# Two chunks at a time on TensorE: order h, o, h, o, then scores of both, y of both, k times v of both, with the scores in four PSUM banks

## The chip, the cores and the metric

The kernel runs on one core of a Trainium2 chip. The metric is the device time of one execution in microseconds; the median of three runs is given. A profile of one further execution goes with it. PE is TensorE, DVE is VectorE, ACT is ScalarE, POOL is GpSimd, and SP is the engine whose queue issues nearly all DMAs here.

## The reference

A linear attention with a decaying state (RWKV-5) is followed by a feed-forward block with a SoLU and a layer norm. All is float32. Sizes: B = 4, H = 8, S = 768, D = 48; 3072 tokens of H x D = 384 features, d_ff = 1024.

```python
for t in range(S):                                   # per batch and head
    cur = einsum('bhd,bhe->bhde', u[None] * k[t], v[t])
    y[t] = einsum('bhd,bhde->bhe', r[t], state + cur)
    state = w * state + einsum('bhd,bhe->bhde', k[t], v[t])
x = y as (B * S, H * D)
h = x @ w_in                                         # 384 -> 1024
sm = exp(h - max(h)) / (sum(exp(h - max(h))) + 1e-9)
solu = h * sm
ln = (solu - mean(solu)) / sqrt(var(solu) + 1e-6) * g_ln
out = ln @ w_out                                     # 1024 -> 384
```

## The kernel before

The tokens are cut into chunks of T = 128: six per batch, four batches, so N = 24 chunks (`units`). Chunk n belongs to batch n mod 4, so two neighbouring chunks never share a state. All work is in `direct_path`; a second function, `general_path`, stands behind a flag that the checks compute and is not executed with these inputs.

The order of instructions is written out by hand (`tc.manual_schedule()`): each engine executes its own instructions in the order in which the Python code issues them. The main loop runs over i, and each iteration does steps of several chunks in a pipeline: attention of chunk i, scores of chunk i + 1, preparation of chunks i + 2 and i + 3, the first product of chunk j = i - 2 (LA = 2) and the output product of chunk l = i - 7 (LO = 5).

What one chunk needs, with the names that are used below:

- `load`: DMAs of k, r and v, on SP, with 192 KB each.
- POOL: `decay_k` makes kp (L674), `decay_r` makes rp (L681), `weigh` makes rku (L687, L688), the state's multiplication by the decay (L785), and two small steps in `deviation`.
- Turned k and r (rk): up to chunk 8 by transposes on PE (`turn_r` L710, `turn_k` L718, the copies on DVE L711 and ACT L720). From chunk 9 (FIRST = 9) as 16-bit halves: `halve_rk` splits kp on ACT (L859) and rp on DVE (L860), a transposing DMA on SP (`turn`, L834) moves them, and `join_rk` joins them on DVE (L839, rk).
- `sum_own` (DVE L692) makes own, and `diagonal` (ACT L698, eight activations) writes the diagonal of AT.
- `scores` (PE L733): 16 matmuls into the PSUM tile at (two banks), then one predicated copy into AT on DVE (L735).
- `finish`: y on PE (L760; a part from the state and rk, then a part from AT and v), the copy xT on ACT (L772), kv on PE (L778), and the state's addition on DVE (L784). The last chunk of each batch (i = 20 to 23) needs no kv.
- `ffn_in` (PE L795, 6 products with 512 columns into the two banks of h_ps, then the exponential e on ACT, L798) and `unit`: reciprocal (DVE L805), e times h (DVE L807, which reads h_ps last), two passes on ACT (L809 and the squares L810).
- `halve_ln` (ACT L845), the transposing DMA, `join_ln` (DVE L839, lnT), and `ffn_out` (PE L877, 8 products with 384 columns, copy o on ACT L879, output DMA on SP L880).

The first iterations also convert the float64 weights in 14 pieces (`load_weights` L506, `convert_a` to `convert_d`). Later, the pieces are loaded again for a check of their size: `load_weights` on SP, then `check_words` in the next iteration, an absolute value on ACT (mag, L558) and a minimum on DVE (least, L560). Before the change, one piece is handled in each iteration from i = 12 on. `check_range` reads w once and compares it on DVE (L641 to L644). `check_sums` combines all checks ahead of the last output product; its product n_ps (L658) goes to PE.

[...]Before, at has two, h_ps two, and four single-bank buffers of pool psM rotate over turned r, turned k, o_ps, y_ps and kv_ps. Halves and reloaded pieces share one SBUF pool tag with six buffers (raw).

In the main stretch (i from 8 on) the order on PE is h, o, scores, y, kv:

```python
        if not early:
            if j < N and not early_h:
                ffn_in(j)
            if i + 2 < N:
                diagonal(i + 2)
            if j < N and not early_h:
                unit(j)
            if l == N - 1:
                check_sums()
            ffn_out(l)
        if 0 <= i + 1 < N:
            scores(i + 1)
        ...
        if 0 <= i < N:
            finish(i)
```

Of the kernel before, what the change touches and what calls it, by code (L numbers as in the profile page):

```python
# [399 lines left out]
def direct_path(  # L400
# [28 lines left out]
    T = 128  # L429
# [20 lines left out]
    psH = ctx.enter_context(tc.tile_pool(name="psH", bufs=1, space=PSUM))  # L450
    psM = ctx.enter_context(tc.tile_pool(name="psM", bufs=4, space=PSUM))

# [32 lines left out]
    for i in range(NLD):  # L485
        nc.vector.memset(kpads[i][:, :, D:P], 0.0)
        nc.vector.memset(rpads[i][:, :, D:P], 0.0)
    pss = psA.tile([128, 2, HP, T], F32, name="at")
    nc.vector.memset(pss, 0.0)

# [125 lines left out]

    def turn_table(table, out):
        ps = psM.tile([128, HP, 128], F32, tag="m", name="kd_ps")
        for a in range(HP):
            nc.tensor.transpose(ps[:, a, :], table[:, a, :], ident)  # L620
        nc.scalar.copy(out=out, in_=ps)  # L621
# [49 lines left out]
    def decay_k(i):  # L671
        X = live.setdefault(i, {})
        X["kp"] = apool.tile([128, H, P], F32, name="kp", bufs=4)
        nc.gpsimd.tensor_mul(X["kp"].rearrange("p h d -> p (h d)"),  # L674
                             kpads[i % NLD].rearrange("p h d -> p (h d)"),
                             kdec.rearrange("p a d -> p (a d)"))
# [29 lines left out]
    def turn_r(i):  # L706
        rT = factors(i)["rT"]
        ps = psM.tile([128, HP, T], F32, tag="m", name="tr_ps")
        for a in range(HP):
            nc.tensor.transpose(ps[:, a, :], pair(rpads[i % NLD], a), ident)  # L710
        nc.vector.tensor_mul(rT, ps, fore)  # L711

    def turn_k(i):
        X = live[i]
        ps = psM.tile([128, HP, T], F32, tag="m", name="tk_ps")

        for a in range(HP):
            nc.tensor.transpose(ps[:, a, :], pair(X["kp"] if i > 0 else kpads[0], a), ident)  # L718
        if i > 0:
            nc.scalar.copy(out=X["kT"], in_=ps)  # L720
        else:
            nc.vector.tensor_mul(X["kT"], ps, back)
# [3 lines left out]
    def scores(i):  # L726
        X = live[i]
        A4 = X["AT"].rearrange("p (a q) t -> p q a t", q=2)
        for a in range(HP):
            for c in range(2):  # L730
                for q in range(2):
                    rows = slice(q * P, q * P + D)
                    nc.tensor.matmul(pss[ts(c, P), q, a, c * P :], X["kT"][rows, a, ts(c, P)],  # L733
                                     X["rT"][rows, a, c * P :], start=True, stop=True)
        nc.vector.copy_predicated(A4, later.unsqueeze(1).to_broadcast([128, 2, HP, T]), pss)  # L735

# [11 lines left out]

    def finish(i):
        b, c = units[i]  # L750
# [18 lines left out]
        for n, (m, h, at) in enumerate(inner):  # L769
            into(m, vf[:, at : at + 32], AT[:, h, :], last[m] == n)  # L770
        X["xT"] = fpool.tile([128, KD, 128], F32, name="xT", bufs=LA + 1)
        nc.scalar.copy(out=X["xT"], in_=y_ps)  # L772
        if c < C - 1:
            kv_ps = psM.tile([128, HP, D], F32, tag="m", name="kv_ps")
            for a in range(HP):
                for g in range(4):
                    h = 2 * a + g // 2
                    nc.tensor.matmul(kv_ps[ts(g, 32), a], X["kp"][:, h, ts(g % 2, 32)],  # L778
                                     vt[:, h, 0:D], start=True, stop=True)
            for q in range(2):  # L780
                wT = pw[ts(q, P), 0, 7].unsqueeze(2).to_broadcast([P, HP, D])
                S = St[ts(q, P), :, q]
                if c > 0:
                    nc.vector.tensor_add(S, kv_ps[ts(q, P)], S)  # L784
                    nc.gpsimd.tensor_mul(S, S, wT)  # L785
                else:
                    nc.vector.tensor_mul(S, kv_ps[ts(q, P)], wT)


    def ffn_in(i):  # L790
        X = live[i]
        h_ps = psH.tile([128, dff], F32, tag="h", name="h_ps")
        for n in range(dff // NX):
            for j in range(KD):
                nc.tensor.matmul(h_ps[:, ts(n, NX)], X["xT"][:, j, :], w_in_sb[:, j, ts(n, NX)],  # L795
                                 start=(j == 0), stop=(j == KD - 1))
        e = X["e"] = fpool.tile([128, dff], F32, name="e")
        nc.scalar.activation(out=e, in_=h_ps, func=ACT.Exp, accum_out=sums[:, i : i + 1])  # L798
# [87 lines left out]
    now = []  # L886
    for i in range(-2, N + LA + LO):
        j, l = i - LA, i - LA - LO
        early = l < 0
        if i == -1:  # L890
            nc.sync.dma_start(out=g_sb, in_=moe_g_ln.rearrange("(c p) -> p c", p=128))
        if 0 <= i and i + 5 < N:
            load(i + 5, "kr")
        if 0 <= i and i + 3 < N:
            load(i + 3, "v")
        early_h = l <= 0
        if early_h and i >= LA:
            ffn_in(j)
# [4 lines left out]
        if i == -2:  # L903
            turn_r(0)
            turn_k(0)
            turn_table(back, kdec)
            weigh(0, nc.vector)
            decay_k(0)
            sum_own(0)
        for p in now:  # L910
            convert_a(p)
            if ahead < len(pieces):
                load_weights(ahead)
                ahead += 1
        if -2 < i and i + 2 < N:
            if i + 2 < FIRST:
                turn_r(i + 2)
            elif not early_h:
                join_rk(i + 2)
            if early_h and i >= LA:  # L920
                unit(j)
            if early_h and i + 2 >= FIRST:
                join_rk(i + 2)
            if i < 0 or i >= LA:
                sum_own(i + 2)
            if i + 2 < FIRST:
                turn_k(i + 2)
        if i < LA:
            for p in now:
                convert_b(p)  # L930
        if i == 0:
            sum_own(2)
        if i + 3 < N and i != 1:
            decay_k(i + 3)
# [6 lines left out]
        if i == 1:  # L941
            weigh(3, nc.gpsimd)
            decay_k(4)
        if 1 <= i and i + 3 < N:
            weigh(i + 3, nc.gpsimd)
        if 0 <= j - 1 < N:
            deviation(j - 1)
        if i == 10:
            check_range()
        if 12 <= i < 12 + len(pieces):  # L950
            load_weights(i - 12)
        if 13 <= i < 13 + len(pieces):
            check_words(i - 13)
        if 0 <= l + 2 < N:
            halve_ln(l + 2)
        if 0 <= l + 1 < N:
            join_ln(l + 1)
        if i + 3 < N:
            halve_rk(i + 3)
        if not early:  # L960
            if j < N and not early_h:
                ffn_in(j)
            if i + 2 < N:
                diagonal(i + 2)
            if j < N and not early_h:
                unit(j)
            if l == N - 1:
                check_sums()
            ffn_out(l)
        if 0 <= i + 1 < N:  # L970
            scores(i + 1)
        if i < 0:
            diagonal(i + 2)
        if 0 <= i < N:
            finish(i)
        if i == 1:
            turn_table(fore, rdec)
            sum_own(3)
        if early and 0 <= i:
            diagonal(i + 2)  # L980
        if i == 1:
            nc.vector.tensor_single_scalar(out=minus_g, in_=g_sb, scalar=-1.0, op=ALU.mult)
        if i >= LA:
            for p in before:
                convert_d(p)
            for p in now:
                convert_b(p)
    return bad

# [41 lines left out]
```

## Time and profile before

| what | value |
|---|---|
| median of 3 runs | 354.58 us (354.47 to 355.15) |
| the profiled execution | 355.35 us, of which its span is 353.5 us |
| granted TensorE clock | 0.997 |
| instructions in the span | 8407 |
| DMA | 52.75 MB, mean 149 GB/s |
| first h product | 27.63 us from the span's start |
| first o product (i = 7) | 78.33 us |
| start of the last h (chunk 23) | 311.28 us |
| end of the last o product | 347.92 us |

The profile gives for each engine the time in which it was busy. Idle time of an engine costs something only where the engine that ends last has to wait for it. So the views to read are the chain that ended last, the timeline of PE with its idle times, and the timelines of the other engines in the stretch concerned. In a timeline a row shows the start, the duration, the engine, the line, what is written and read, the number of instructions, and in brackets how long the engine was idle before and what ended that. A PE product shows twice as many matmul records as the code has, and neighbouring groups overlap by a little, since matmuls are pipelined; a group's share is read from start to start.

### The profile page before, as it was taken

The page shows a single profiled execution, that of the slowest core. Times are in us where ns is not written, and L with a number is a line of the kernel's source. Part 1 is how long each engine was busy: PE and PEld are TensorE (multiplying, and loading weights), DVE is VectorE, ACT ScalarE, POOL GpSimd, SP SyncE. Part 2 cuts the span into 40 slices and gives each one's busy share as a digit, 9 for nine tenths or more (in the row PEclk, how much of TensorE's full clock was granted, in tenths as well). Part 3 has the DMA queues.
Part 4 walks back from the last instruction along what each step waited for, and adds up shares of the span by engine and source line. Part 5 has one row for each costly group of instructions (what it writes and reads, how often), then busy time and mean ns, then how long its engine had stood idle before and what let it go on. Part 6 is the DMA issues. An engine that isn't in the chain of part 4 may idle for free.

```text
span 353.5 us, 8407 instructions
## 1 busy us (share of the span) xinstructions
PE 338.0 (96%) x3427; PEld 204.8 (58%) x3427; DVE 210.8 (60%) x323; ACT 242.1 (68%) x457; POOL 176.5 (50%) x196
## 2 busy tenths in 40 slices
PE   2699999999999999999999999999999999999993
PEld 2485566656566556566566566565565565555563
DVE  7795888886468567665865765765771441323220
ACT  3765988988897667677867778778687464465510
POOL 3879667784865754945945846746730000000000
PEclk9999999999999999999999999999999999999998
DMA  7998997259999868988997979857663523551641
GB/s 164 266 237 183 252 209 126 51 105 162 189 186 163 150 122 154 195 174 185 188 159 174 206 146 184 187 130 146 150 129 62 126 69 59 128 126 47 139 105 33
DMA packets 164878, 52.75 MB, mean 149 GB/s; under 512 B 157917, under 2 KB 161246, under 8 KB 164830
## 3 DMA queue, kind: packets, MB, share of 16 engines
q1 hardware_dynamic: 164686, 51.92, 71.9%
q8 instruction: 29, 0.48, 0.6%
q10 hardware_dynamic: 144, 0.20, 0.2%
q14 instruction: 19, 0.16, 0.2%
HBM read 26.94 MB, written 4.72 MB: 90 GB/s over the span
## 4 chain that ended last, share of the span: by engine, by line
PE 90%; issue 3%; POOL 2%; DVE 2%; ACT 1%; DMA 1%; POOLq 0%; DVEq 0%
PE o_ps L877 35%; PE h_ps L795 35%; PE y_ps L760 10%; PE at L733 6%; PE kv_ps L778 2%; PE tk_ps L718 1%; PE tr_ps L710 1%; POOL kp L674 1%; DMA wq<-in_w_dram 1%; ACT AT L698 1%; POOL rku L687 1%; DVE part L530 0%; DVE ma L532 0%; POOL w_in_sb L540 0%; DVE solu L807 0%
## 5 line engine op out<-in xcount | busy, mean ns | idle before, releaser
L795 PE MATMUL h_ps<-w_in_sb,xT 128*128 128x512 f32 x288 | 129.8, 600 | 0.7 <-DVE solu L807 0.5
L877 PE MATMUL o_ps<-w_out_sb,lnT 128*128 128x384 f32 (+1 forms) x400 | 127.3, 473 | 0.0
L877 PEld LDWEIGHTS o_ps<-w_out_sb,lnT 128*128 128x128 f32 x400 | 75.1, 190 | 52.8 <-issue 9.1
L795 PEld LDWEIGHTS h_ps<-w_in_sb,xT 128*128 128x128 f32 x288 | 52.8, 190 | 60.7 <-issue 58.1
L698 ACT ACTIVATE AT<-ident,own 128x128 f32<-128x128 f32 x192 | 58.6, 391 | 6.2 <-DVE own L692 6.2
L785 POOL TENSOR_TENSOR state<-state,pw 64x192 f32<-64x192 f32 x32 | 25.6, 800 | 63.2 <-DVE state L784 62.0
L735 DVE COPY_PREDICATED AT<-later,at 128x1024 f32<-128x1024 uint32 x24 | 31.9, 1329 | 31.4 <-PE at L733 31.4
L845 ACT COPY halves<-solu 128x2048 uint16<-128x2048 uint16 x24 | 45.4, 1893 | 0.0
L839 DVE COPY lnT<-halves 128x2048 uint16<-128x2048 uint16 x24 | 37.4, 1559 | 11.7 <-DMA halves<-halves 11.7
L809 ACT ACTIVATE solu<-solu,st 128x1024 f32<-128x1024 f32 x24 | 27.5, 1148 | 22.6 <-DVE solu L807 22.6
L798 ACT ACTIVATE e<-h_ps 128x1024 f32<-128x1024 f32 x24 | 24.5, 1021 | 18.3 <-PE h_ps L795 18.3
L816 POOL TENSOR_SCALAR st<-st 128x1 f32<-128x1 f32 x24 | 7.0, 292 | 59.2 <-ACT e L810 59.2
L674 POOL TENSOR_TENSOR kp<-kpad,kdec 128x512 f32<-128x512 f32 x24 | 31.6, 1317 | 7.6 <-ACT kdec L621 6.5
L807 DVE SCALAR_TENSOR_TENSOR solu<-h_ps,st,e 128x1024 f32<-128x1024 f32 x24 | 30.8, 1284 | 2.5 <-DVE st L805 0.5
L688 POOL TENSOR_TENSOR rku<-rku,rpad 128x384 f32<-128x384 f32 x23 | 28.9, 1256 | 1.8
L839 DVE COPY rk<-halves 128x2048 uint16<-128x2048 uint16 x15 | 21.7, 1444 | 11.4 <-DMA halves<-halves 11.0
L733 PE MATMUL at<-rk 48*64 48x128 f32 (+1 forms) x768 | 27.9, 265 | 0.0
L733 PEld LDWEIGHTS at<-rk 48*64 48x64 f32 x768 | 21.8, 139 | 10.4 <-issue 8.8
L681 POOL TENSOR_TENSOR rp<-rpad,rdec 128x512 f32<-128x512 f32 x15 | 27.4, 1829 | 0.0
L860 DVE COPY halves<-rp 128x1024 uint16<-128x1024 uint16 x15 | 19.8, 1319 | 11.3 <-POOL rp L681 11.3
L760 PE MATMUL y_ps<-AT,vt 128*32 128x128 f32 x768 | 26.3, 279 | 0.0
L810 ACT ACTIVATE e<-solu 128x1024 f32<-128x1024 f32 x24 | 25.4, 1057 | 0.8
(82 smaller groups left out, 320.3 us busy)
## 6 DMA issues: line engine op xcount, KB each, us to landing
raw<-in_moe_w_in_dram SPq DMA_DIRECT2D x12, 512.0 KB, 5.7
raw<-in_moe_w_out_dram SPq DMA_DIRECT2D x16, 384.0 KB, 4.7
kpad<-in_k_dram SPq DMA_DIRECT2D x24, 192.0 KB, 4.2
rpad<-in_r_dram SPq DMA_DIRECT2D x24, 192.0 KB, 4.6
vt<-in_v_dram SPq DMA_DIRECT2D x24, 192.0 KB, 4.5
out_dram<-o SPq DMA_DIRECT2D x23, 192.0 KB, 2.2
halves<-halves SPq DMA_TRANSPOSE x39, 4.6
u_bc<-in_u_dram ACTq DMA_DIRECT2D x1, 192.0 KB, 3.8
```

The lines of the kernel that those rows point to most:

```text
L674: nc.gpsimd.tensor_mul(X["kp"].rearrange("p h d -> p (h d)"), kpads[i % NLD].rearrange("p h d -> p (h d)"), kdec.rearrange("p a d -> p (a ...
L688: engine.tensor_mul(rku, rku, rpads[i % NLD][:, :, 0:D])
L698: nc.scalar.activation(out=AT[:, h, :], in_=ident, func=ACT.Copy, scale=X["own"][:, h])
L733: nc.tensor.matmul(pss[ts(c, P), q, a, c * P :], X["kT"][rows, a, ts(c, P)], X["rT"][rows, a, c * P :], start=True, stop=True)
L735: nc.vector.copy_predicated(A4, later.unsqueeze(1).to_broadcast([128, 2, HP, T]), pss)
L760: nc.tensor.matmul(y_ps[32 * g : 32 * g + 32, j, :], lhsT, rhs, start=(g not in opened), stop=stop, skip_group_check=True)
L795: nc.tensor.matmul(h_ps[:, ts(n, NX)], X["xT"][:, j, :], w_in_sb[:, j, ts(n, NX)], start=(j == 0), stop=(j == KD - 1))
L807: nc.vector.scalar_tensor_tensor(out=solu, in0=X["h"], scalar=rs, in1=X["e"], op0=ALU.mult, op1=ALU.mult, accum_out=tot)
L809: nc.scalar.activation(out=solu, in_=solu, func=ACT.Identity, scale=-float(dff), bias=tot)
L839: nc.vector.tensor_copy(out=words.bitcast(U16).rearrange("p n (t o) -> p o n t", o=2), in_=turned)
L845: nc.scalar.copy(out=both.rearrange("p (o n) -> p o n", o=2), in_=split(X["solu"]))
L877: nc.tensor.matmul(o_ps, X["lnT"][:, f, :], w_out_sb[:, f, part], start=(f == 0), stop=(f == KF - 1))
```

## The change

The loop is cut in two. Up to i = 6 it goes on as before, one chunk at a time. From i = 7 (LA + LO, the first output product) a second loop steps by two: both chunks of a pair are handled in one iteration. On PE the order is then h, o, h, o, scores of chunks i + 1 and i + 2, y of chunks i and i + 1, kv of both.

The scores of the two chunks go to two tiles of two banks each, so four banks. The second tile also takes the turned r and k of the first loop, one bank each. psM shrinks from four buffers to two, which serve o_ps, y_ps and one kv_ps for both chunks. kp has five buffers in place of four, e has one in place of two. `scores` and `finish` are taken apart into what is on PE and what is behind it.

On the other queues the steps are regrouped: both pairs of loads, both joins of rk, both own sums and all of POOL's work for two chunks stand at the head of an iteration; the halves, diagonals and joins of ln are placed around the two h and o. At i = 7 (`late`) the join of rk for chunk 9 stands behind the first unit. The reloads of weights for the check are no longer one per iteration: four are issued at the end of the iterations i = 21, 23 and 25, two at the end of i = 27, and they are checked at the head of the next iteration. `check_range` moves from i = 10 to i = 9.

The core of the diff (lines of the functions' bodies that stay are left out):

```diff
-    psM = ctx.enter_context(tc.tile_pool(name="psM", bufs=4, space=PSUM))
+    psM = ctx.enter_context(tc.tile_pool(name="psM", bufs=2, space=PSUM))
...
-    pss = psA.tile([128, 2, HP, T], F32, name="at")
-    nc.vector.memset(pss, 0.0)
+    pss = [psA.tile([128, 2, HP, T], F32, name=f"at{n}") for n in range(2)]
+    nc.vector.memset(pss[0], 0.0)
...
     def turn_r(i):
-        ps = psM.tile([128, HP, T], F32, tag="m", name="tr_ps")
+        ps = pss[1][:, 0]
...
     def turn_k(i):
-        ps = psM.tile([128, HP, T], F32, tag="m", name="tk_ps")
+        ps = pss[1][:, 1]
...
     def scores(i):
+        ps = pss[i % 2 if i > LA + LO else 0]
...
+        X["scores"] = ps
+
+    def take_scores(i):
+        A4 = live[i]["AT"].rearrange("p (a q) t -> p q a t", q=2)
+        nc.vector.copy_predicated(A4, later.unsqueeze(1).to_broadcast([128, 2, HP, T]),
+                                  live[i]["scores"])
...
-    def finish(i):
+    def heads(i):
...
+        X["y"] = y_ps
+
+    def take_y(i):
+        X = live[i]
         X["xT"] = fpool.tile([128, KD, 128], F32, name="xT", bufs=LA + 1)
-        nc.scalar.copy(out=X["xT"], in_=y_ps)
+        nc.scalar.copy(out=X["xT"], in_=X["y"])
+
+    def outer(chunks):
...
+        kv_ps = psM.tile([128, 2, HP, D], F32, tag="m", name="kv_ps")
...
-        e = X["e"] = fpool.tile([128, dff], F32, name="e")
+        e = X["e"] = fpool.tile([128, dff], F32, name="e", bufs=1)
...
-    for i in range(-2, N + LA + LO):
+    for i in range(-2, LA + LO):
...
+    checks, checked = list(range(len(pieces))), []
+    for i in range(LA + LO, N + LA + LO, 2):
+        j, l = i - LA, i - LA - LO
+        for n in (i, i + 1):
+            if n + 5 < N:
+                load(n + 5, "kr")
+            if n + 3 < N:
+                load(n + 3, "v")
+        new = [n for n in (i + 1, i + 2) if FIRST <= n < N]
+        late = i == LA + LO
+        for n in new if not late else []:
+            join_rk(n)
+        for n in new:
+            sum_own(n)
+        for n in (i + 3, i + 4):
+            if n < N:
+                decay_k(n)
+                decay_r(n)
+                weigh(n, nc.gpsimd)
+        for n in (j - 2, j - 1):
+            if LO - 1 <= n < N:
+                deviation(n)
+        for p in checked:
+            check_words(p)
+        if i == LA + LO + 2:
+            check_range()
+        for half in range(2):
+            if l + half + 2 < N:
+                halve_ln(l + half + 2)
+            if half == 0 and new:
+                diagonal(new[0])
+            if l + half + 1 < N:
+                join_ln(l + half + 1)
+            if j + half < N:
+                ffn_in(j + half)
+                unit(j + half)
+            if late and half == 0:
+                join_rk(new[0])
+            if i + half + 3 < N:
+                halve_rk(i + half + 3)
+            if half == 0 and len(new) > 1:
+                diagonal(new[1])
+            if l + half == N - 1:
+                check_sums()
+            ffn_out(l + half)
+        now = [n for n in (i + 1, i + 2) if n < N]
+        for n in now:
+            scores(n)
+        for n in now:
+            take_scores(n)
+        now = [n for n in (i, i + 1) if n < N]
+        for n in now:
+            heads(n)
+            take_y(n)
+        outer(now)
+        for n in now:
+            update(n)
+        checked, checks = (checks[:4], checks[4:]) if i >= N - 3 else ([], checks)
+        for p in checked:
+            load_weights(p)
```

## The prediction

> **What bounds the kernel now.** First the page: busy shares, then the chain that ended last.
>
> ```profile
> PE 338.0 (96%) x3427; PEld 204.8 (58%) x3427; DVE 210.8 (60%) x323; ACT 242.1 (68%) x457; POOL 176.5 (50%) x196
> PE 90%; issue 3%; POOL 2%; DVE 2%; ACT 1%; DMA 1%; POOLq 0%; DVEq 0%
> ```
>
> PE is busy all the time and is the chain. Then the timeline of PE: one unit of the main stretch (h, o, scores, y, kv, next h), and the end, where an o is followed by an h.
>
> ```profile
> 154.38 5.42 PE L795 MATMUL h_ps<-w_in_sb,xT 128*128 128x512 f32 x12
> 159.63 5.32 PE L877 MATMUL o_ps<-w_out_sb,lnT 128*128 128x384 f32 x16
> 164.88 1.09 PE L733 MATMUL at<-rk 48*64 48x128 f32 x32
> 165.90 0.86 PE L760 MATMUL y_ps<-rk,state 128*32 128x128 f32 x24
> 166.58 1.06 PE L760 MATMUL y_ps<-AT,vt 128*32 128x128 f32 x32
> 167.46 0.52 PE L778 MATMUL kv_ps<-vt,kp 128*32 128x48 f32 x32
> 167.91 5.42 PE L795 MATMUL h_ps<-w_in_sb,xT 128*128 128x512 f32 x12
> ...
> 306.12 5.32 PE L877 MATMUL o_ps<-w_out_sb,lnT 128*128 128x384 f32 x16
> 311.28 5.31 PE L795 MATMUL h_ps<-w_in_sb,xT 128*128 128x512 f32 x12
> 316.43 25.96 PE L877 MATMUL o_ps<-w_out_sb,lnT 128*128 128x384 f32 x80
> ```
>
> Each group starts where the one before stops: a unit takes 167.91 - 154.38 = 13.53 us and PE waits for nothing. So two things can move the time: less PE work at the borders of groups, and any new wait that reaches PE. From 27.6 to 348 us PE now loses only 0.6 us to waits.
>
> The rows that I use for the other queues, from the timeline of all engines (seam of the loops; h to the unit's squares; weight check and join near the end), the issues of the reload line, and a half-microsecond window in which one reload moves:
>
> ```profile
> 78.41 2.45 ACT L698 ACTIVATE AT<-ident,own 128x128 f32<-128x128 f32 x8
> 80.75 1.01 ACT L798 ACTIVATE e<-h_ps 128x1024 f32<-128x1024 f32 x1
> ```
> ```profile
> 294.15 1.02 ACT L798 ACTIVATE e<-h_ps 128x1024 f32<-128x1024 f32 x1 [2.51 <-PE h_ps L795]
> 295.56 1.28 DVE L807 SCALAR_TENSOR_TENSOR solu<-h_ps,st,e 128x1024 f32<-128x1024 f32 x1
> 296.89 1.15 ACT L809 ACTIVATE solu<-solu,st 128x1024 f32<-128x1024 f32 x1 [1.63 <-DVE solu L807]
> 298.07 1.06 ACT L810 ACTIVATE e<-solu 128x1024 f32<-128x1024 f32 x1
> ```
> ```profile
> 289.21 0.55 ACT L558 ACTIVATE mag<-raw 128x384 f32<-128x384 f32 x1
> 289.75 1.89 ACT L845 COPY halves<-solu 128x2048 uint16<-128x2048 uint16 x1
> 289.88 0.55 DVE L560 TENSOR_REDUCE least<-mag 128x1 f32<-128x384 f32 x1 [1.37 <-ACT mag L558]
> 290.35 1.32 DVE L839 COPY lnT<-halves 128x2048 uint16<-128x2048 uint16 x1
> ```
> ```profile
> L506 SPq DMA_DIRECT2D raw<-in_moe_w_out_dram x1: 424/424/424, 312.5 to 312.5; - x1
> DMA to landing us min/median/max: 3.3/3.3/3.3
> ```
> ```profile
> 313.00:313.50 0.50, 0.50 (x3) 0.26 (x2) 0.50 (x2) 0.50 (x1) 0.00 (x0) 1.00 0.94 350
> ```
>
> Read from them: from the start of e to the start of the L809 pass is 2.74 us, h_ps being free 0.05 us before; L809 to L810 is 1.18, L810 to the next 1.06. A second reload behind a first costs 0.39 MB / 350 GB/s = 1.1 us (0.52 MB: 1.5).
>
> **What the Trainium skill says.** "TensorEngine Tiling (Array Packing)", Key Properties: changing the tiling mode drains TensorE. The trace agrees, at a small price (below). "TensorE: Matmul & The Clock Gate", Architectural detail: ScalarE and VectorE are strict FIFO. It agrees: the e at 80.75 belongs to an h that ended at 78.33 and starts 2.34 after the AT group ahead of it, the group's pace. "DMA: Bandwidth & Descriptors", Queues, rings and completion order: a DMA engine takes the descriptors of a ring in order; I rely on it for a transpose with loads behind it, which no view of before shows.
>
> **The change, part by part.** n is a chunk; T is where the first h of a pair starts on PE.
>
> *Borders.* Per pair one border of each kind goes. o before h instead of scores: 311.28 - 306.12 = 5.16 against 5.25, 0.09. h after o: 5.15 against 5.25, 0.10. Scores then y: weight loads of y stand 0.17 on issue, so the second scores cost an estimated 0.85. Second kv: by columns from y's AT part (0.88 for 128 columns), 0.33 against 0.45, 0.12. Second y: 0.03. That is 0.39 for 8 pairs (i = 7 to 21) and 0.12 for the 6 with two kv: **-3.8 us**. Bounds: o streams 8 x 384 columns in 5.16, 1.68 ns each; at that rate the columns of scores (512 deep on four tiles), y (896) and kv (192) take 2.69 of their 3.03 us, so with the 0.19 at o and h all borders of a unit cost 0.53: at most 4.3. At least 2, if only half is saved.
>
> *Pair in steady state.* PE now needs 5.25 + 5.16 + 5.15 + 5.25 + 1.87 + 3.1 + 0.8 = 26.55. ACT and DVE in program order, with rows of before: kv ends at T; four state adds to T+1.6, two rk joins to 4.2, own 4.7; AT group 4.75 to 7.1; e (h ready at 5.4), L809 at 9.85, h_ps free at 9.8, needed at 10.4, so the second h is not held. L810 11.0, kp halves 12.1, second AT group 13.1, o 15.5, ln halves 16, e 17.75, L809 20.5, L810 21.7, kp halves 22.7, o 23.8 to 24.3. The second y takes the bank of that o: psM has two. PE would start it at 20.8 + 1.87 + 1.55 = 24.2, so it waits until 24.4: **0.2 us** in each of 5 pairs, +1.0. Behind it in ACT are both xT (0.48 each). The scores' four banks hide both L735 copies (1.34 each) beside y. POOL's four state multiplies and two chunks of kp, rp and rku, about 18 us, end by T+18, ahead of their readers. e with one buffer costs nothing: ACT writes e after its own squares in either order. In the first loop, PE's order is the same, and turned r and k have a bank each: nothing.
>
> *Seam, i = 7.* In the old code e of chunk 5 came right behind the AT group (80.75). In the new one ln halves (1.8) and another AT group (2.34) are queued ahead: e starts at 84.9, h_ps is free at 87.6. h of chunk 6 now comes after one o, at 73.07 + 5.25 + 5.16 = 83.5: PE stands **4.2 us**. This is the first of two large terms. In i = 9 the range check's reads of w (0.56 + 0.34 + 0.55 + 0.54 on DVE) stand before join and reciprocal: +0.5.
>
> *xT of chunk 23, i = 23.* No kv or second y lies between its y and its h: 0.25 + 0.48 + 0.1, **+0.85**.
>
> *End.* The weight checks used to be one reload per unit. Now fours are loaded by SP behind the second out of i = 21, 23 and 25, two behind i = 27, and read at the top of the next pair, ahead of the ln joins on DVE and the ln halves on ACT. Those of i = 21 land by T+4.5 and hold nothing. Let T now be the start of the last h (chunk 23). Reloads 4 to 7 are issued at T-1.2 and land at T+6.2 (3.3 and three more). mag 6.9, ln halves of 20 8.7, e, L809 11.4, L810, o, ln halves of 21 to 16.0, its transpose (1.8 on SP), out of 19, reloads 8 to 11 issued at 18.3, landed at 24.9. mag 25.6, the four least 26.2, only then join of 21, 27.5: o of 21, due at 5.25 + 3 x 5.16 = 20.7, starts 6.9 late. It ends at 32.7, its out is issued at 33.5, reloads 12 and 13 behind it land at 38.3; mag 39.0, least 39.6, join of 23 40.9, the sums 41.8; n_ps, then o of 23 at 42.1 against 31.2 undelayed: **+11 us**. Bounds: if the four land as fast as SP can issue them, 6; at half the rate, 17.
>
> Sum on the profiled execution's own 355.35: -3.8 + 1.0 + 4.2 + 0.5 + 0.85 + 11.0 = +13.75, 369.1. The median of before is 0.77 below that execution: **368.3**.
>
> **Rivals.** (a) Reloads overlap better: end +6, 363. For: 16 engines take a piece in about 1 us. Against: each piece still waits for the out before it. (b) The transpose of the second rk of a pair, issued at 2.9 before T, has the next loads behind it and lands 7.8 later (the slowest seen with loads ahead; alone 4.3 to 4.6): 2.0 too late for its join at T+2.9, and own, AT group, e, o and the second y all wait: +2.0 in 5 pairs, 378. Against: order in the ring. (c) Faster: work that is ready passes work that waits in the queues of ACT and DVE. Then e passes the ln halves and AT group at the seam, the joins pass mag and least, and 4.2 + 0.5 + 1.0 + 11.0 = 16.7 go: 352.4 on the profiled execution, 351.6. It decides from 13.75 of these 16.7 on. Against: the e at 80.75, held 2.3 us by a group that had nothing to do with it. (d) The change does not do what it says: the new order of PE is h, o, h, o, scores twice, y twice, kv twice, so no.
>
> **How the numbers follow.** Main case 0.75, 368.3, own range 364.5 to 373. (a) 0.1, (b) 0.1, (c), or a tie from several errors, 0.05. The range 362 to 377 takes in (a) and nearly (b). About 0.2% is what a measurement of this kernel tells from no change. Faster 0.03, same 0.02, slower 0.95.
>
> **What would show it.** Right: PE of i = 9 to 21 at about 26.6 to 26.9 a pair; an idle of about 4 before the second h of the first pair, released by L807's successor; near the end PE idle before o of 21 and of 23, released by the lnT join, which itself waited behind least for mag and the reloads. Wrong: no idle at the end, or idle in every pair behind rk joins.

## The result, and where the time went

After the change the median is 391.02 us (390.15 to 392.94) against 354.58, four runs of each: 1.103 times the time before, 95% interval 1.099 to 1.108. The forecast was 368.3 with a range up to 377: the direction was right, but of 36.4 us of loss it saw 13.7, and the measured time lies far outside the range. The profiled execution took 390.42 us, with a span of 388.6 us (before 355.35 and 353.5).

First the page, the shares of busy time and the row of the granted clock in 40 slices:

```profile
PE 343.5 (88%) x3427; PEld 207.5 (53%) x3427; DVE 212.9 (55%) x323; ACT 242.3 (62%) x457; POOL 179.6 (46%) x196
PEclk9989999998998799999999999999999999996888
```

TensorE was busy for 96% of the span before and is for 88% now. It is also busy for 5.5 us more, 343.5 against 338.0, with the same 3427 products: the clock row has an 8 in the tenth slice, 87 in the thirteenth and fourteenth, and 6888 at the end. So there is idle time, and there are products that run slowly. The view of waits, for TensorE (what waited, for what, us in total, times, the longest), names the idle time:

```profile
PE o_ps L900 <- DVE lnT L862: 9.0, 1, 9.0
PE at L718 <- DVE rk L711: 8.8, 7, 2.5
PE h_ps L818 <- DVE solu L830: 7.8, 3, 4.4
PE n_ps L658 <- DVE low L656: 3.5, 1, 3.5
```

The second row is in the first loop, which was not meant to change, and the third is in i = 7, 9 and 23. The steady pair isn't there. Its timeline shows why (start, duration, engine, line, operation, idle before):

```profile
198.64 5.42 PE L818 MATMUL h_ps<-w_in_sb,xT 128*128 128x512 f32 x12
...
222.03 1.06 PE L765 MATMUL y_ps<-AT,vt 128*32 128x128 f32 x32
223.07 0.86 PE L765 MATMUL y_ps<-rk,state 128*32 128x128 f32 x24
...
225.42 1.12 PE L818 MATMUL h_ps<-w_in_sb,xT 128*128 128x512 f32 x2
```

225.42 - 198.64 is 26.78 us for two chunks, where before it was 2 x 13.53 = 27.06: pairing gains 0.3 us a pair. The second y starts at 223.07, 1.04 us behind the second part of the first one; in i = 7 these starts lie 0.88 apart (107.39 and 108.27). So it waits 0.16 us; the o copy on ScalarE that frees its bank runs from 222.36 to 222.93.

Starts of the same products in both timelines, subtracted, give the account (us of the span, after less before):

| stretch | change |
|---|---|
| up to the first o (85.01 against 78.33) | +6.7 |
| i = 7, to the h of chunk 7 (110.59 against 100.27) | +3.6 |
| i = 9, to the h of chunk 9 (145.08 against 127.31) | +7.5 |
| i = 11 to 21, to the h of chunk 21 (304.55 against 288.70) | -1.9 |
| i = 23, to the last h (329.03 against 311.28) | +1.9 |
| from the last h to the end of the last o (53.12 against 36.64) | +16.5 |
| behind the last o | +0.9 |

But for rounding they come to 35.1, the difference of the spans. The rows behind the large terms follow. In the first loop turned k waits. The first row is from before, where turned r started at 32.88; the second is the same product after the change, where turned r started at 34.40:

```profile
33.32 0.60 PE L718 MATMUL tk_ps<-ident,kp 128*128 128x128 f32 x4
...
35.94 0.63 PE L718 MATMUL at<-ident,kp 128*128 128x128 f32 x4 [0.94 <-DVE rk L711]
```

In i = 9 the timeline of all engines shows VectorE's range check ahead of the reciprocal that h waits for, and GpSimd's multiplications beside it:

```profile
117.96 1.00 POOL L687 TENSOR_TENSOR rku<-kpad,u_bc 128x384 f32<-128x384 f32 x1
118.03 1.14 DVE L641 TENSOR_SCALAR ok<-wrow 1x384 f32<-1x384 f32 x1 [2.04 <-DMA wrow<-in_w_dram]
119.04 1.00 POOL L688 TENSOR_TENSOR rku<-rku,rpad 128x384 f32<-128x384 f32 x1
119.10 1.15 DVE L642 TENSOR_SCALAR ok<-wrow 1x384 f32<-1x384 f32 x1
119.99 1.38 POOL L674 TENSOR_TENSOR kp<-kpad,kdec 128x512 f32<-128x512 f32 x1
120.28 1.50 DVE L643 TENSOR_TENSOR ok<-ok,ok 1x384 f32<-1x384 f32 x1
123.97 0.14 DVE L828 RECIPROCAL st<-sums 128x1 f32<-128x1 f32 x1
```

e had been ready since 118.9. The four operations took 0.56 + 0.34 + 0.55 + 0.54 before; now the first three take 1.14 + 1.15 + 1.50 (the reduction that follows took 0.54 both times), and they start only after 2.04 us of waiting for w's row. That wait is not new. Before, VectorE stood longer for the row, and no product of TensorE waited for it:

```profile
120.60 0.56 DVE L641 TENSOR_SCALAR ok<-wrow 1x384 f32<-1x384 f32 x1 [4.15 <-DMA wrow<-in_w_dram]
```

What is new is the room behind it: before, the next h came 13.5 us after the one ahead, now the second h of a pair is due after 10.4.

At the end the chain of the forecast is there, from the timeline of all engines: reloads, mag, join, o of 21.

```profile
349.19 1.88 SPq L507 DMA_DIRECT2D raw<-in_moe_w_out_dram  x4
353.52 0.54 ACT L559 ACTIVATE mag<-raw 128x384 f32<-128x384 f32 x1 [6.89 <-DMA raw<-in_moe_w_out_dram]
...
357.62 1.31 DVE L862 COPY lnT<-halves 128x2048 uint16<-128x2048 uint16 x1
...
359.08 2.26 PE L900 MATMUL o_ps<-w_out_sb,lnT 128*128 128x384 f32 x3 [8.97 <-DVE lnT L862]
```

And last the slow products, from the busy times by stretch (behind the five engines' columns stand the granted clock, the DMA share and the GB/s):

```profile
92.60:96.00 3.40, 3.38 (x4) 1.33 (x5) 2.58 (x2) 3.37 (x5) 3.18 (x3) 0.54 1.51 165
125.60:129.00 3.40, 3.40 (x4) 1.47 (x5) 2.16 (x2) 3.37 (x5) 3.16 (x5) 0.50 0.00 0
359.00:362.50 3.50, 3.42 (x6) 1.94 (x7) 0.00 (x0) 2.18 (x2) 0.00 (x0) 0.50 0.75 142
```

These three windows stand right behind idles of 2.29, 4.39 and 8.97 us, and the clock in them is about half. From start to start the second h of i = 7 took 6.95 us where a full one takes 5.15 (+1.8), that of i = 9 7.64 (+2.5), the o of 21 and 22 12.25 where two take 10.4 (+1.85), and the last o, behind the idle of 3.55, 7.15 where it took 5.47 (+1.7). That is 7.9 us in which TensorE counts as busy.

### The profile page after: what moved, and what is told of

Same layout as the page of the kernel before. It is cut to its first block, busy times and chain, and to the rows that moved or that the text cites. A ratio compares the mean times of both kernels' runs of the same rounds, so it can differ in the third digit from the quotient of the medians.

```text
span 388.6 us, 8449 instructions
## 1 busy us (share of the span) xinstructions
PE 343.5 (88%) x3427; PEld 207.5 (53%) x3427; DVE 212.9 (55%) x323; ACT 242.3 (62%) x457; POOL 179.6 (46%) x196
## 5 line engine op out<-in xcount | busy, mean ns | idle before, releaser
L818 PE MATMUL h_ps<-w_in_sb,xT 128*128 128x512 f32 x288 | 133.3, 614 | 8.4 <-DVE solu L830 7.8
L900 PE MATMUL o_ps<-w_out_sb,lnT 128*128 128x384 f32 (+1 forms) x400 | 131.0, 484 | 9.0 <-DVE lnT L862 9.0
L900 PEld LDWEIGHTS o_ps<-w_out_sb,lnT 128*128 128x128 f32 x400 | 77.5, 196 | 63.3 <-issue 10.6
L698 ACT ACTIVATE AT<-ident,own 128x128 f32<-128x128 f32 x192 | 58.7, 390 | 26.6 <-DVE own L692 26.6
L808 POOL TENSOR_TENSOR state<-state,pw 64x192 f32<-64x192 f32 x32 | 29.4, 919 | 83.5 <-DVE state L807 81.9
L832 ACT ACTIVATE solu<-solu,st 128x1024 f32<-128x1024 f32 x24 | 27.6, 1150 | 40.1 <-DVE solu L830 40.1
L862 DVE COPY lnT<-halves 128x2048 uint16<-128x2048 uint16 x24 | 41.5, 1728 | 15.5 <-DMA halves<-halves 14.7
L828 DVE RECIPROCAL st<-sums 128x1 f32<-128x1 f32 x24 | 3.9, 163 | 56.7 <-ACT e L821 56.7
L561 DVE TENSOR_REDUCE least<-mag 128x1 f32<-128x384 f32 (+1 forms) x14 | 8.5, 610 | 35.4 <-ACT mag L559 35.4
L688 POOL TENSOR_TENSOR rku<-rku,rpad 128x384 f32<-128x384 f32 x23 | 26.0, 1129 | 1.8
L733 PE MATMUL at<-rk 48*64 48x128 f32 (+1 forms) x768 | 25.4, 261 | 0.0
L687 POOL TENSOR_TENSOR rku<-kpad,u_bc 128x384 f32<-128x384 f32 x23 | 25.2, 1094 | 0.0
```

The source lines that it names most:

```text
L698: nc.scalar.activation(out=AT[:, h, :], in_=ident, func=ACT.Copy, scale=X["own"][:, h])
L832: nc.scalar.activation(out=solu, in_=solu, func=ACT.Identity, scale=-float(dff), bias=tot)
L862: nc.vector.tensor_copy(out=words.bitcast(U16).rearrange("p n (t o) -> p o n t", o=2), in_=turned)
L900: nc.tensor.matmul(o_ps, X["lnT"][:, f, :], w_out_sb[:, f, part], start=(f == 0), stop=(f == KF - 1))
```

## Experiments

The theory was: four places, each with its own cause (turned r and k in one tile; the order on ScalarE at the seam; the range check; the reloads in fours), and a clock that falls behind each idle. The rivals were that pairing has a cost of its own, in banks or DMA, and that the clock has another cause. All ratios are to the kernel before, measured again beside each run, with 95% intervals; the change itself stands at 391.0 us and 1.103.

### One edit at a time

Turned r takes a rotating bank again:

```diff
     def turn_r(i):
-        ps = pss[1][:, 0]
+        ps = psM.tile([128, HP, T], F32, tag="m", name="tr_ps")
```

> The change with one edit: in the first loop turned r takes a bank of the rotating pool again, so it no longer shares a tile with turned k. Theory (the 6.7 us lost before the first o come from TensorE's turned k waiting for VectorE's multiply of turned r, because both lie in one tile): these waits go, o of chunk 0 starts near 78.4 us instead of 85.0, and 6 to 7 us go from the total: 384. Rival A (the loss comes from having two rotating banks where there were four): o of chunk 0 stays near 85, total unchanged. Rival B (ScalarE, not TensorE, sets the pace up to the seam): o of chunk 0 starts earlier but the wait before the second h of i = 7 grows by as much, total down by 3 at most.

Measured: 386.0 us, 1.090 (1.083 to 1.097). The o of chunk 0 starts at 78.17, and turned k no longer waits for turned r:

```profile
41.97 0.60 PE L718 MATMUL at<-ident,kp 128*128 128x128 f32 x4
```

It starts at 41.97, behind turned r at 41.53, as before the change. So the wait came from the shared tile, though r and k lay in different banks of it; rival A is out, as the pool still had two banks. The gain on the median, 5.0 us, is less than the 6 to 7 expected. The wait before the second h of i = 7 grew from 2.29 to 3.64 us, which is rival B's effect, at a fifth of the gain.

The reloads go two to a pair:

```diff
-        checked, checks = (checks[:4], checks[4:]) if i >= N - 3 else ([], checks)
+        checked, checks = (checks[:2], checks[2:]) if i >= LA + LO + 2 else ([], checks)
```

> The change with one edit: the 14 reloads of the weight check go two to a pair from i = 9 to 21, in place of four to a pair from i = 21 on. Theory (the tail is reloads that land late, and the checks and joins queued behind them): the idles of 9.0 before o of 21 and 3.5 before n_ps go with their slow clock, and the last o ends about 37 us after the last h starts instead of 53; 16 to 18 us go, total 373 to 375, and a pair of the main stretch stays within 0.3 of 26.8. Rival A (the ln transposes with outs behind them set the tail): less than 5 go. Rival B (reloads among the transposes delay the joins of every pair): pairs grow by 0.5 to 1 us and half of the gain is given back, total 380.

Measured: 396.4 us, 1.116 (1.111 to 1.121): slower than the change. The tail did what the theory said: the last h starts at 351.80, the last o ends at 388.91, 37.1 us later instead of 53.1. But the pairs that read reloads, i = 11 to 21, take 28.0 to 33.4 us. The first mag of a pair says why, on ScalarE's timeline:

```profile
212.74 0.68 ACT L559 ACTIVATE mag<-raw 128x512 f32<-128x512 f32 x1 [3.59 <-DMA raw<-in_moe_w_in_dram]
```

The reload was issued from 208.28 on and read at the head of the next pair. ScalarE stood for it, and ln halves, AT group and e behind it. This is neither the theory nor rival B as written: not the transposes were late, but the mag at the head of a queue.

So the same spreading was tried with the check further back (`check_words` behind the first unit of the pair):

> The change with two edits: reloads two to a pair from i = 9 to 21, and their checks on ScalarE and VectorE placed behind the first unit of the next pair instead of at its head. Theory (spreading alone lost because mag, at the head of ScalarE's queue, waited 3.6 us and then 1.1 for reloads issued only 4 us before, and AT group, e and solu stood behind it): read 10 us later the reloads have landed, no pair has an idle before its second h, pairs stay at 26.8, the tail stays as short as in the spread run (last o ends 37 us after the last h starts), total down by 16 from the change: 375. Rival (16 transfers more in the ring among the transposes delay the joins themselves): idles of 1 to 3 stay in the pairs of i = 11 to 21, total 382 or more.

Measured: 378.65 us, 1.067 (1.065 to 1.069). No h waits in the pairs from i = 11 on, and the tail is 37.1 again. The reloads in fours cost 16 us, as the theory said; 12.4 of them come back on the median. A new wait stands against it: the second y of a pair stands 1.2 us, five times, for the bank of the o that ScalarE has not copied yet; the two mags are now ahead of that copy.

The range check's row is loaded in i = 9, and compared in i = 25 (the DMA is taken out of `check_range`):

```diff
         if i == LA + LO + 2:
-            check_range()
+            nc.sync.dma_start(out=wrow, in_=w.rearrange("h d -> (h d)").partition_broadcast(1))
+        if i == N + 1:
+            check_range()
```

> The change with one edit: the row of w for the range check is loaded in i = 9 as now, but VectorE compares it in i = 25. Theory (the 4.4 us of idle and the slow clock after it in i = 9 are VectorE standing at w's row and then in four slow operations on it, ahead of join, reciprocal and solu): the idle before the second h of i = 9 goes, i = 9 falls from 34.5 to about 27, total down by 7: 384. Rival A (VectorE is late in i = 9 from the backlog of the seam, whatever the check does): an idle of 2 or more stays, total down by 2 to 3. Rival B (the comparison stalls the end just as much): what i = 9 gains is lost in i = 25.

Measured: 383.9 us, 1.079 (1.073 to 1.084). i = 9 takes 26.81 us instead of 34.49: 7.7 us for four operations on one partition and the wait for their row, of which 4.4 were idle time and 2.5 the slow clock behind it. Rival B holds for 1.6 us: in i = 25 the second o waits for a join that stands behind the comparisons. In i = 25 no GpSimd operation runs beside them, and the same operations are short:

```profile
331.62 0.34 DVE L639 TENSOR_SCALAR ok<-wrow 1x384 f32<-1x384 f32 x1
332.26 0.55 DVE L641 TENSOR_TENSOR ok<-ok,ok 1x384 f32<-1x384 f32 x1
```

The rows of i = 9 in the change tell more than that the operations are long. Each of the first three ends just behind the GpSimd multiplication that was running when it began: at 119.17 behind 118.96, at 120.25 behind 120.04, at 121.78 behind 121.37. In all six profiles that have the check in i = 9, 18 times in all, the lag is 0.20 to 0.22 us with one input and 0.40 or 0.41 with two, while the durations go from 0.49 to 1.50. So these operations were not slowed in proportion; they lasted until the multiplication was done. The reduction was not held: it took 0.54 with a multiplication running from its start to its end.

At the seam, the first h and its unit go first:

```diff
+            if late and half == 0:
+                ffn_in(j)
+                unit(j)
             if l + half + 2 < N:
                 halve_ln(l + half + 2)
```

> The change with one edit: in i = 7 the first h and its unit are issued ahead of the ln halves and of the first AT group. Theory (the 2.3 us of idle before the second h of i = 7 and the slow clock after it come from e being queued behind these on ScalarE): the idle goes, and i = 7 gives back 3.6 to 4.1 us; the later joins may return up to 2 of it in i = 9, total down by 2 to 4: 387 to 389. Rival A (ScalarE brings a backlog from the first loop, and e is late in any order): idle of 2 stays, total unchanged. Rival B (the ln halves that are now later make o of the next pair wait): the idle moves to the joins of i = 9, total unchanged or up.

Measured: 391.9 us, 1.106 (1.100 to 1.112): no gain. Yet the idle in i = 7 was gone, and i = 7 took 28.43 instead of 30.84. In i = 9 the idle grew from 4.39 to 6.41: w's row was there at 119.08, where it had been at 118.03, so VectorE waited 4.99 us for it. What the seam gained, the next wait took. Whether that is so, both edits together must show:

> The change with two edits: in i = 7 the first h and unit ahead of the ln halves and the first AT group, and the range check's comparisons moved to i = 25. Theory (the order of the seam alone gave nothing because VectorE then waited longer for w's row, which lands at the same time, 119.1 against 118.0): with the range check away the two gains add, 7 and 2 to 4, and i = 7 and i = 9 together take 55 to 57 us instead of 65.3: total 379 to 381. Rival (the seam's idle is a backlog of ScalarE and only moves): i = 9 keeps an idle of 2, total 383.5 as with the range check alone.

Measured: 381.9 us, 1.078 (1.075 to 1.081). In the profile i = 7 and 9 take 28.45 + 26.78 = 55.2 us, against 65.3 in the change, so the idle did not merely move. Against the profile with the range check alone (30.84 + 26.81) the seam is worth 2.4. On the medians it is 2 us, which is within the scatter: the runs with the range check alone went from 380.4 to 384.5 us.

### The clock

27 products that nobody reads were put into TensorE's idles, in front of the product that waits:

```diff
+    fills = {(LA + LO, 1): 3, (LA + LO + 2, 1): 6, (27, 1): 13, (29, 1): 5}
...
+            for n in range(fills.get((i, half), 0)):
+                nc.tensor.matmul(fill, ident, w_out_sb[:, 0, :], start=True, stop=True)
```

> The change with products of no use put into TensorE's four largest idles: 3 before the second h of i = 7, 6 before that of i = 9, 13 before o of 21, 5 before n_ps, each 128x384 of about 0.64 us into a bank that nobody reads then; no wait is changed. Theory (the granted clock falls to a half for about 3.4 us after an idle of 2.3 us or more, and this costs 1.8 + 2.5 + 1.85 + 1.7): the waits' ends stay where they are, the second h of i = 7 and 9 and the o of 21 take 5.3 to 5.4 us at full clock, total down by 5 to 8: 383 to 386. Rival A (the clock falls for another reason, by power or by the time of the run): the slow stretches stay and the total is unchanged. Rival B (more work throttles TensorE elsewhere): total up.

Measured: 384.5 us, 1.083 (1.079 to 1.086). More work on TensorE, 6.5 us less time, and a mean granted clock of 0.994 instead of 0.962. The o of 21 runs at full speed, and so does that of 22 behind it, 5.40 from 363.17 on:

```profile
357.46 5.40 PE L900 MATMUL o_ps<-w_out_sb,lnT 128*128 128x384 f32 x16 [0.80 <-DVE lnT L862]
```

Only in i = 9 an idle of 2.58 was left, and the h behind it was slow again, 6.81 us instead of 5.15; 7.9 less these 1.7 is 6.2, about what went. So these idles of TensorE cost twice, once while it waits and once behind it. Rivals A and B are out.

### All four, and what was left

> The change with all four edits: turned r in the rotating pool, first h and unit first in i = 7, the range check's comparisons in i = 25 behind the unit, reloads spread and read behind the first unit. Theory (these four are the whole loss, and pairing itself gains the 0.3 us a pair that steady pairs show): 391 less 6.8, 2 to 4, 7.7 and 16 to 17, that is 355 to 358, at a granted clock back near 1.0; at best before less 2. Rival A (pairing has a cost of its own, in banks or in the ring, that the single edits hid): 362 or more with idles at other places. Rival B (the four overlap): the sum of the parts is not reached because a new wait follows each.

Measured: 364.4 us, 1.027 (1.024 to 1.029), clock 0.991. The four edits take back 26.6 of the 36.4 us. The theory's 355 to 358 was missed, and rival A is right for most of the rest. One row of the waits carries it:

```profile
PE y_ps L763 <- ACT o L900: 9.1, 6, 3.0
```

The second y of a pair needs the bank of the second o, since only two banks rotate: 3.0 us in i = 7, where ScalarE is late, and 1.2 on the mean in the pairs that check weights.

To free that bank early, the second o copy was put ahead of the kp halves on ScalarE (in i = 7 on VectorE, the second argument of `ffn_out`), and reloads got two buffers of their own, issued behind the first o and read behind the next pair's first ln halves (for room, mag uses ma's buffers, and one comparison overwrites w's row):

```diff
-            ffn_out(l + half)
+            ffn_out(l + half, late and half == 1)
+            if half == 1 and i + half + 3 < N:
+                halve_rk(i + half + 3)
+            if half == 0:
...
+                for p in now_checks:
+                    load_weights(p, "chk", 2)
```

> All four edits, and three more against the wait that is left, the second y of a pair standing for the bank that the second o's copy on ScalarE has not left yet (3.0 us in i = 7, 1.3 in each pair with a weight check, 9.1 in all; two of its slow starts cost 1.5 more): that copy comes ahead of the kp halves on ScalarE, in i = 7 it goes to VectorE, and the reloads get two buffers of their own, are issued half a pair earlier and read behind the first ln halves, where ScalarE waits for own. Theory (this wait is the rest of the loss, and pairing itself gains): no y waits over 0.3, pairs with checks fall from 28.1 to 26.6, i = 7 falls from 31.6 to 27.5, total 352 to 355, a tie with before or up to 0.7% faster. Rival A (two banks in the pool hold pairs up somewhere else): pairs stay above 27.1, total 358 or more. Rival B (with the reloads issued in mid pair the transposes behind them land late): idles released by lnT or rk joins, total 360.

Measured: 359.1 us, 1.013 (1.010 to 1.017): 5.3 of the 9.6 us that were left. No y waits for a copy of o any more, and the pair of i = 13 takes 26.58. But the 352 to 355 of the theory were missed: i = 9 took 30.0, and single h waited up to 1.4 us. Was the first pair in the wrong place, next to the busy first loop?

> As the run before it, but i = 7 and 8 go one at a time in the old order and the pairs begin at i = 9 in the order of the change (the o copy of i = 7 is on ScalarE again). Theory (what was left, 4 us against before by the start of the h of i = 11, is the seam: pairs begin while ScalarE still carries the backlog of the first loop): i = 7 and i = 8 take 13.5 each, i = 9 falls from 30.0 to 26.6 or at most 28, one pair's gain of 0.45 is lost, total 354.5 to 356.5, a tie. Rival A (any first pair costs 2 to 4 wherever it stands, since its joins start late): i = 9 stays near 30, total 358. Rival B (two rotating banks hold up the single units, kv waiting for the o copy): i = 7 and 8 take 14 or more, total 357.

Measured: 364.2 us, 1.026 (1.023 to 1.029). i = 9 fell to 27.8, but with two banks the single units of i = 7 and 8 stall: kv of i = 7 waited 5.5 us for the o copy, rival B. With i = 7 in another order:

> As the run before it, with i = 7 ordered so that its bank is free in time: h and unit first, then the rk join, then the o copy on VectorE, and only then the ln halves and the AT group. Theory (the 5.5 us before kv of i = 7 were the o copy on ScalarE behind e, which was behind ln halves, kp halves and, through solu, the rk join; with the slow start after it and the late i = 8 they cost 7.7): kv does not wait, i = 7 takes 13.6 and i = 8 13.6 to 14, total 355 to 357 on the median, a tie within 0.5% with before. Rival (the join of rk of chunk 9 lands late in any order and holds the scores or the AT group of i = 8): i = 8 takes 15 or more, total 358 or more.

Measured: 360.7 us, 1.016 (1.013 to 1.018). i = 7 took 14.1, but kv of i = 8 waited 2.5 us for its o copy and i = 9 started slowly behind it. The wait moved by one unit. So the pool got its four banks back, with one tile for the scores (2 + 2 + 4 banks, as before the change):

```diff
-    psM = ctx.enter_context(tc.tile_pool(name="psM", bufs=2, space=PSUM))
+    psM = ctx.enter_context(tc.tile_pool(name="psM", bufs=4, space=PSUM))
...
         for n in now:
+            if n + 1 < N:
+                scores(n + 1)
+                take_scores(n + 1)
             heads(n)
             take_y(n)
```

> The kernel of the run with banks freed early, but scores keep one tile of two banks, as before the change, so the rotating pool has four again (turned r and k both from it), and the order of a pair is h, o, h, o, scores, y, scores, y, kv of both. Theory (what is left over before, about 4 us, all lost by the h of chunk 9, comes with the two-bank pool, through y and kv waiting for ScalarE's or VectorE's copies): no y or kv waits for a copy, i = 7 falls from 28.7 to 27 to 27.5 and i = 9 from 30.0 to 27 to 28.5, steady pairs are 26.6 to 26.8 since the borders of scores and y come back (0.1), total 354 to 356, a tie. Rival (what is left is the seam's late work on ScalarE and the joins behind it, not the banks): i = 7 and 9 keep 58 together and the total stays at 358 to 360.

Measured: 360.4 us, 1.014 (1.013 to 1.016), the same as with two. No product waits for a bank of the pool any more. In its place, the scores of the second chunk wait 1.9 us in i = 7 until VectorE has copied those of the first out of the one tile. And the pair of i = 17 takes 28.6, its second h waiting 1.5 us for solu. The second join of rk on VectorE's timeline shows what is late there:

```profile
216.76 1.82 DVE L860 COPY rk<-halves 128x2048 uint16<-128x2048 uint16 x1 [1.61 <-DMA halves<-halves]
```

Its transpose was issued at 209.67, behind the o copy, with loads close behind it; joins of rk wait 3.4 us in four places (4.3 in five in the run with banks freed early, which has the same edit). This is rival (b) of the forecast, brought in by the edit that was to free the bank. Undone, with the four banks kept:

> The kernel of the run with four rotating banks, with two of its edits undone: the kp halves of a pair's second chunk come ahead of the o copy on ScalarE again, and the o copy of i = 7 is on ScalarE again (with four banks nobody waits for these copies). Theory (of the 5 us that are left over before, 3 to 4 are h waiting 1.4 to 1.5 for solu in single pairs because the second rk transpose, issued behind the o copy, lands late and holds join, own, AT group and e): rk joins wait for no transpose in the main stretch, no h waits over 0.3, pairs are 26.6 to 26.9, total 356 to 357.5. Rival A (the transposes are late from the reloads put into mid pair, not from the order on ScalarE): the idles stay, total 360. Rival B (all of the rest is the seam, i = 7 and 9): both stay at 57 together and the total at 358 to 360 though the later idles go.

Measured: 357.4 us, 1.0068 (1.0055 to 1.0082), within 0.1% from run to run, and inside the 356 to 357.5 expected. The transposes of that pair are issued from 201.6 on, joins of rk wait 0.4 us in all, and steady pairs take 26.87. What is left is at the seam, as rival B had it: i = 7 takes 28.6 and i = 9 28.2 where two units took 27.2 and 27.0. In i = 7 the wait for the one scores tile is left in the view of waits:

```profile
PE at L731 <- DVE AT L737: 1.4, 1, 1.4
```

None of these versions beats the kernel before; the best is 0.7% slower. It loses about 2.5 us at the seam and 0.6 on the last h, which waits for xT, and gains 0.2 a pair.

## Why the forecast was wrong, and what in it was right

The forecast was 22.7 us too low. Its large mechanisms, the seam, the end and the gain of a pair, were right. Three steps failed: the first loop was put at nothing, the range check at +0.5, and no idle was charged for the slow clock behind it. The end was too small as well, in part by the same clock.

- **Borders and y's bank: right.** A pair of 26.75 was forecast (the parts as printed add up to 26.58 and not to 26.55), 26.78 was measured, with a y wait of 0.16 where 0.2 was said.
- **Seam: the mechanism and nearly the size, by two errors that cancel.** 4.2 us of idle were forecast (87.6 less 83.5 is 4.1). With the first loop as forecast (the run with its own bank) it was 3.64; in the change it was 2.29, because TensorE came 6.7 us late itself, plus 1.8 for a clock that was not in the sum. That the sum fits is luck.
- **"In the first loop ... turned r and k have a bank each: nothing" failed.** It cost 6.7 us. A bank each was not enough: inside one tile turned k waited until VectorE had read turned r, and with turned r in a tile of its own it did not. Whether the program asks for this wait because of the shared tile, or the chip would need it with two banks of one tile, wasn't tried.
- **"In i = 9 the range check's reads ... +0.5" failed.** It was 7.5 us of which the forecast had 0.2 net. The operations' durations came from rows of before, where GpSimd's multiplications ended as the second of them began. Grouping two chunks puts its eight multiplications for both right there: 1.14 + 1.15 + 1.50, each lasting until the multiplication beside it was done, against 0.34 + 0.34 + 0.55 with none beside them in i = 25. The Trainium skill ("GPSIMD Engine Reference", Key points) says that GpSimd shares its SBUF interfaces with VectorE and contends with some of its instructions; the trace agrees, and the reduction with 0.54 both times is one that did not contend here. And the wait for w's row, 2.04, was not in the sum: the check's DMA is issued behind six loads. The trace of before had it, with 4.15, where it cost nothing.
- **End: the mechanism right, 11.0 for 16.5.** The o of 21 started 30.05 us behind the last h where 27.6 was forecast, and n_ps at 45.85 where it was 42.1. 3.55 of the 5.5 that are missing are the slow clock; the other 2 are reloads that land later, the first four at 7.4 where 6.2 was said, the next four at 27.5 where it was 24.9. "Those of i = 21 land by T+4.5 and hold nothing" failed too: they landed at 6.3, and h of chunk 22 waited 1.1 us.
- **The clock was in no term.** It made 7.9 of the 36 us. The Trainium skill ("TensorE: Matmul & The Clock Gate", Part 1) says that TensorE falls to half its clock when it was idle for about 3.4 us, and needs about as long of work to come back. The forecast had idles of 4.2 to 7 in it and priced none of them so. The windows at 0.50 to 0.54 agree with it, and full clock came back 3.4 to 4.4 us into the work in i = 7, 4.4 to 5.4 in i = 9; the idle that is enough was shorter here (below).

First loop 6.7, range check 7.2 (7.45 less 0.2), end 6.4 with the 0.9 behind it, h of 22 1.1, seam -0.1 (3.6 for 3.7 with its borders): that is the 21.3 us between forecast sum and profiled execution. Of the rivals, (a) is refuted by the tail, (b) by the joins of rk, which waited 0.7 us in all, and (c) by every queue above; (d) was none.

## What to carry to other kernels

Where work is grouped, read what stands next in each in-order queue, and take durations and landing times from rows with the same neighbours: a check that cost nothing in a free unit cost 7.7 us in a full one. Price an idle of TensorE of 2.5 us or more at its length plus about 2 us behind it (1.5 to 2.8 in these runs), and count two halves of one tile as one buffer until a trace shows otherwise. Mend such a change with all its edits together, since one wait taken away may only let the next one show: the seam alone gave nothing, and with the range check away 2.4 us in the profile.

## What the hardware showed that was not expected

- From i = 7 on, idles of 1.94 us and less left the clock alone in all these runs, and those of 2.5 and more brought it to about half each time. Between 2.2 and 2.4 us both happen: an idle of 2.29 before the second h of i = 7 in the change did it (0.54), one of 2.28 in the run with spread reloads did not (1.00), with the same products around it.
- Three small operations of VectorE (one partition, 384 elements) lasted until 0.2 us behind the end of the GpSimd multiplication that ran when they began, 0.4 us with two inputs, 18 times of 18. So their time followed GpSimd's operation: with one input 0.34 us alone and 0.49 to 1.42 beside a multiplication. A reduction of the same row was not held (0.54).
- kv sometimes stands for 0.6 to 1.5 us for nothing that the profile shows, mostly in the first two pairs. What it is stays open; no run was made on it.
